# An RWKV-7 recurrence with a feed-forward network: the state's growth from weights of 40 columns, and the inverse decays turned ahead of minus x

## The chip, the cores and the metric

The kernel runs on one core of one Trainium2 chip. The metric is device time in microseconds (us) of one execution, the median of several runs. The engines are TensorE (PE, whose weight loads have a row of their own, PEld), VectorE (DVE), ScalarE (ACT), GpSimd (POOL) and SyncE (SP), which here only issues DMAs.

## The reference

A recurrence over 768 time steps for 4 batches and 8 heads of 40 elements, then a feed-forward network on its output:

```python
for t in range(S):
    kt, vt, rt = (k[:, :, t], v[:, :, t], r[:, :, t])
    wt, at, bt = (w[:, :, t], a[:, :, t], b[:, :, t])
    y[:, :, t] = np.einsum('bhd,bhde->bhe', rt, state)
    Sa = np.einsum('bhde,bhe->bhd', state, at)
    state_decay = state * wt[:, :, None, :] - np.einsum('bhd,bhe->bhde', Sa, bt)
    state = state_decay + np.einsum('bhd,bhe->bhde', vt, kt)
...
h = np.maximum(x @ w_in, 0.0)          # x: (3072, 320), w_in: (320, 2048)
return (h * h @ w_out)                 # w_out: (2048, 320)
```

The recurrence's inputs are 32-bit floats. The two weight matrices are 64-bit floats, which the kernel rounds to 32 bits on VectorE and ScalarE in its opening.

## The kernel before

**Chunks and slots.** Time is cut into 6 chunks of 128 steps for each of 4 batches: 24 chunks, numbered so that the batch runs fastest. Within a chunk the recurrence becomes matrix products: with cumulated decays (`dec`, its parts UP, DOWN and A) the inner dependence is a triangular system, which GpSimd inverts ahead of time (`solving`, results kept in memory and loaded as `T` or `blocks`). Heads go in pairs: a head has 40 elements, and a pair takes 128 partitions, the second head starting at 64 (`DP = 64`), so that 24 columns or rows after each head are padding. The tiles `in_k`, `in_v`, `in_b` and `minus_x` hold 8 heads of 64 columns of which 40 carry data and the rest are zeros.

**The chain of a chunk** (`chain`) is a generator whose steps the planner spreads among other work. Minus x is solved in two halves (`times_t`, copied to `minus_x` by ScalarE on line 658, two copies for each half). Then minus x is turned by four transposes on TensorE (line 671) into a bank of the pool ps_c, copied by ScalarE (line 673) to `xnT`, multiplied with `rT` and masked to `RX`. At the end come y (the products named RV,in_k and RX,in_b) and, for chunks 0 to 19, the state's growth: for each of 8 heads a product of v-side data (`in_v`) with weights `in_k`, and of `minus_x` with weights `in_b`, added in a bank `grown` of the pool ps_w (the profile names it ps_w). VectorE adds it to the state (line 701). The profile lists every matmul that goes through the helper `mm` under line 87, and each of these f32 matmuls as two loads and two matmuls; a transpose is one of each.

**The order.** Chunks 0 to 6 run in an opening whose order is written out as a list of words. From chunk 7 on, `sorted_slot(i, g, ch)` writes one slot for each chunk i: the chain of chunk i, the preparation of chunk j = i + 1 (turn r, v, k; scale k and b by the inverse decays), the decays of chunks further ahead (the generators `one` and `two`, in slots up to 14), and the feed-forward network's matmuls between. The code's order is each engine's order. `step` calls its arguments and then lets the list of delayed stores move on by one (`tick`).

**What the change touches.** `turn_down` (line 582) turns the inverse decays of chunk j by four transposes into a bank of ps_w, and `scale_kb` (line 588, VectorE) reads that bank. In the slot, `step(on(one), on(ch), of(turn_down))` runs a step of `one` (two products on VectorE, lines 387 and 388), then the transposes of minus x, then those of the inverse decays. Next on TensorE come the products of `rT` with the old state (`rT,sd`), 32 x 32 products named spares (slots up to 12), and the products of `rT` with `xnT`. The transposes of k (in_k, line 331) come before.

Of the kernel before, what the change touches and what calls it, by code (L numbers as in the profile page):

```python
# [17 lines left out]
def kernel(  # L18
# [24 lines left out]
    B, H, S, D = r.shape  # L43
# [7 lines left out]
    DP = 64  # L51
# [30 lines left out]
    def psum(pool):  # L82
        name = "ps_" + pool.name[-1]
        return pool.tile([128, 512], FP32, tag=name, name=name)

    def mm(o, l_, r_, start):
        nc.tensor.matmul(o, l_, r_, start=start, stop=True, skip_group_check=True)  # L87
# [4 lines left out]
    def new(name, shape, bufs):  # L92
        return work.tile(shape, FP32, tag=name, name=name, bufs=bufs)
# [4 lines left out]
    def later(fn, steps=2):  # L98
        line.append([steps, fn])

    def tick():
        for entry in line:
            entry[0] -= 1
        while line and line[0][0] <= 0:
            line.pop(0)[1]()
# [12 lines left out]
    class Ring:  # L118
# [6 lines left out]
        def next(self):  # L125
            self.at = (self.at + 1) % len(self.tiles)
            return self.tiles[self.at]
# [215 lines left out]
    def masked(name, bufs, l_, r_):  # L343
        res = []
        for p_ in products(l_, r_):
            t_ = new(name, [128, NP, 128], bufs)
            nc.vector.tensor_tensor(t_, p_, over4(upper), Alu.mult)  # L347
            res.append(t_)
        return res
# [252 lines left out]
    def begin(i, g):  # L602
        g["x"] = loaded.pop(i)
        g["up"], g["aT"] = g["dec"][:, UP], g["dec"][:, A_, :, :C]
# [27 lines left out]
    def chain(i, g):  # L632
        bb, c = order[i]
        st = states.tiles[bb]
        first, second_ = halves
        k_, b_, v_, rT = (g[x] for x in ("k", "b", "v", "rT"))

        x_ = psum(ps_c)[:, :DM].rearrange("t (h d) -> t h d", h=H)
        if c > 0:
            for f in range(2):  # L640
                for q in range(NP):
                    mm(x_[halves[f ^ q % 2], 2 * q:2 * q + 2], g["aT"][:, q, f * HC:(f + 1) * HC], st[:, q, :, :D], f == 0 and q < 2)
        for f in range(2):
            for n, (h, q, e, flip) in enumerate(heads):
                mm(x_[halves[f ^ flip], h], g["A"][e][:, q, f * HC:(f + 1) * HC], v_[:, h, :D], c == 0 and f == 0 and n < 2)
        xr = new("xr", [128, H, D], 1)
        nc.scalar.copy(xr, x_)  # L647
        yield
        T, N = g["T"], g["N"]
        xn = minus_x.next()  # L650

        def times_t(half):
            xs = psum(ps_c)[:, :NP * D].rearrange("p (n d) -> p n d", n=NP)
            for n, (h, q, e, flip) in enumerate(heads):
                rows = halves[half ^ flip]
                mm(xs[rows, n // 2], T[rows, order_of(h)], xr[rows, h], n < 2)
            for flip in range(2):
                nc.scalar.copy(flipped(xn)[halves[half], flip, :, :, :D], by_pair(xs[halves[half ^ flip]]))  # L658

        times_t(0)  # L660
        yield
        for h, q, e, flip in heads:
            mm(x_[halves[1 - flip], h], N[:, order_of(h)], xn[first, h, :D], False)
        for flip in range(2):
            nc.scalar.copy(flipped(xr)[halves[1 - flip], flip], flipped(x_)[halves[1 - flip], flip])
        yield
        times_t(1)
        yield
        p_ = psum(ps_c)
        for q in range(NP):  # L670
            nc.tensor.transpose(p_[:, q * 128:(q + 1) * 128], pair(xn, q), ident)  # L671
        xT = turned("xnT", 1)
        nc.scalar.copy(xT, quads(p_))
        yield
        y_ = quads(psum(ps_c))
        if c > 0:
            sd = g["sd"]
            for q in range(NP):
                mm(y_[:, q], sd[:, q].rearrange("p e d -> p (e d)"), rT[:, q], q == 0)
        yield  # L680
        rx = masked("RX", 2, xT, rT)
        yield

        for m_, rows in ((g["RV"], k_), (rx, b_)):
            for q in range(NP):
                for e in range(2):
                    mm(y_[e * DP:(e + 1) * DP, q], rows[:, 2 * q + e, :], m_[e][:, q], c == 0 and q == 0 and rows is k_)
        if c < NCH - 1:
            grown = psum(ps_w)[:, :NP * D].rearrange("p (q d) -> p q d", q=NP)
            for l_, r_ in ((k_, v_), (b_, xn)):  # L690
                for h in range(H):
                    mm(grown[h % 2 * DP:(h % 2 + 1) * DP, h // 2], l_[:, h, :], r_[:, h, :D], l_ is k_ and h < 2)
        n = i % GB
        if n == 0:
            tokens[i // GB] = new("tokens", [128, NP, GB * C], 2)
        t_ = tokens[i // GB][:, :, n * C:(n + 1) * C]
        nc.vector.tensor_tensor(t_, y_, g["up"][:, :, :C], Alu.mult)  # L697
        if c < NCH - 1:
            for e in range(2):
                rows = slice(e * DP, (e + 1) * DP)  # L700
                nc.vector.tensor_tensor(st[rows, :, e, :D], grown[rows], st[rows, :, e, :D], Alu.add)
            ended[bb] = new(f"end{bb}", [128, NP], 1)
            nc.scalar.copy(ended[bb], g["up"][:, :, C])
        if n == GB - 1:
            t_ = tokens[i // GB]

            def gather():
                for j, row, h, d, m_ in moves:
                    at = (h % 2) * DP + d
                    on_queue[0].dma_start(out=t_[row:row + m_, j], in_=t_[at:at + m_, h // 2])  # L710

            if i < LAID:
                waiting["m", i // GB] = gather
            else:
                later(gather, 1)
                later(lambda: gathered.add(i // GB), 2)
        yield
# [93 lines left out]
    def run(gen):  # L811
        for _ in gen:
            tick()
# [13 lines left out]
    def prepare(i, g=None, apart=False, steps=0):  # L827
        gen = early(i, g, apart)
        for _ in range(steps):
            next(gen)  # L830
            yield
        if i + 1 < len(order) and i + 1 not in early_loaded:
            load_early(i + 1)
        yield from gen
# [142 lines left out]
    def step(*what):  # L977
        for w_ in what:
            w_()
        tick()  # L980

    on = lambda gen: lambda: next(gen, None)

    def sorted_slot(i, g, ch):
        j = i + 1
        more = j < len(order)
        n = ready.setdefault(j, {}) if more else None
        made = [prepare(m_, apart=True) for m_ in ahead.get(i, ())]
        one, two = (made + [iter(()), iter(())])[:2]
        if j in inversions:  # L990
            n["joining"] = inversions.pop(j)
        early_join = more and "joining" in n
        joining = n.pop("joining") if early_join else inverses(j, n) if more else iter(())
        fine = more and unit_of[j] < FINE
        join = on(joining)
        of = lambda fn: (lambda: fn(j, n)) if more else (lambda: None)

        if more and "x" in n:
            n.update(up=n["dec"][:, UP], aT=n["dec"][:, A_, :, :C])
        elif more:  # L1000
            begin(j, n)
        step(second.make_quarter)
        if fine and not early_join:
            join()
        step(of(turn_rv), on(one), on(one))
        fetch_next(j + 1, "r")
        step(second.make_quarter)
        step(on(ch), of(decay_state))
        step(of(make_rv), second.thirds)
        step(on(ch), on(one))  # L1010
        if fine:
            join()
        step(second.whole)
        step(on(ch))
        step(on(one), of(turn_k))
        step(on(one), on(ch), of(turn_down))
        step(on(ch), of(scale_kb))
        if fine:
            join()
        step(on(ch), of(make_a), second.thirds, on(one))  # L1020
        fetch_next(j + 1, "v")
        step(of(turn_state), second.square, second.whole, on(two))
        if not early_join and not fine:
            join()
        run(ch)
        if more:
            begin_chain(j, n)
        loads(j + 1)
        step(second.square, second.make_quarter, on(two), on(two))
        if i in ahead and len(ahead[i]) > 1:  # L1030
            step(on(two), on(two))
        step(second.make_quarter, on(two))
        for gen in (one, two, joining):
            run(gen)

    for i in range(LAID, len(order)):
# [3 lines left out]
        ch = g["chain"]  # L1040
# [39 lines left out]
```

## Time and profile before

| what | value |
|---|---|
| runs shown | 949.51, 950.41, 963.28 us |
| median | 950.41 us |
| span of the profiled execution | 949.3 us |
| mean granted TensorE clock | 0.958 |
| instructions | 22557 |
| DMA | 103.37 MB, mean 109 GB/s |

The page gives the profiled execution's span, from its first to its last instruction, and no other time of it. A span says how long; the chain that ended last says what it was made of; the groups say how often an operation ran and how long one took; the timeline shows one slot instruction by instruction, with the idle time of an engine in brackets and what ended it. A group such as `128*64 128x40` has weights of 128 rows and 64 columns, and 40 moving columns. A TensorE matmul's length is its latency: matmuls overlap, so the distance from start to start tells what one costs in a row of them.

### The profile page before, as it was taken

The numbers are of one execution on the slowest core, as the hardware profiler recorded it, in microseconds if no ns is written. First come the engines' busy times: TensorE is split into PE (matmuls) and PEld (weight loads), VectorE is DVE, ScalarE is ACT, GpSimd is POOL, SyncE is SP. The second block draws the span as 40 slices with busy tenths as digits, with TensorE's granted clock in tenths as the row PEclk, the third lists the DMA queues.
The fourth block names the chain that finished last, engine by engine and source line by source line (L and its number), as shares of the span: only waits on it lengthen the run. The fifth ranks groups of instructions, "written<-read, shape, count | busy, mean of one in ns | idle before, by whom it ended". The sixth has DMA issues, their size and how long they took to land.

```text
span 949.3 us, 22557 instructions
## 1 busy us (share of the span) xinstructions
PE 896.9 (94%) x9116; PEld 719.2 (76%) x9116; DVE 462.1 (49%) x1131; ACT 284.8 (30%) x735; POOL 509.4 (54%) x935
## 2 busy tenths in 40 slices
PE   6578989879999999999999999999999999999998
PEld 4365656758787887888887888888888877887775
DVE  5927548788863355652664455544334331331110
ACT  3033334534532342342342232222221222222111
POOL 4568246064008786318999959999858870000000
PEclk9768988589999999999999999999999999999999
DMA  9788779856868477896846765604484154210000
GB/s 112 124 160 150 163 127 189 193 127 136 173 104 170 85 139 140 168 173 119 137 78 104 122 173 100 121 13 82 91 168 77 24 108 80 44 30 10 12 14 15
DMA packets 253266, 103.37 MB, mean 109 GB/s; under 512 B 234154, under 2 KB 240298, under 8 KB 252010
## 3 DMA queue, kind: packets, MB, share of 16 engines
q1 hardware_dynamic: 244709, 83.00, 49.2%
q0 software_dynamic: 3760, 17.10, 7.5%
q10 hardware_dynamic: 4693, 1.83, 0.9%
q8 instruction: 72, 1.18, 0.6%
q14 instruction: 32, 0.26, 0.1%
HBM read 69.00 MB, written 30.92 MB: 105 GB/s over the span
## 4 chain that ended last, share of the span: by engine, by line
PE 82%; DVE 6%; DMA 3%; ACT 3%; issue 2%; POOL 1%; SPq 1%; ACTq 0%; DVEq 0%; POOLq 0%
PE ps_f L87 40%; PE ps_w L87 17%; PE ps_c L87 14%; PE ps_w L331 5%; PE ps_f L264 2%; PE ps_c L671 2%; PE ps_c L598 1%; PE ps_w L582 1%; SPq L513 1%; DMA kept_q<-N 1%; DMA in_r<-in_r_dram 1%; DMA half_n<-kept_q 1%; ACT N L401 1%; DVE decay L381 1%; DVE decay L380 1%
## 5 line engine op out<-in xcount | busy, mean ns | idle before, releaser
L478 POOL TENSOR_TENSOR half_p<-half_n,half_t 128x462 f32<-128x462 f32 (+39 forms) x406 | 221.9, 547 | 74.3 <-DMA half_n<-kept_q 23.4
L480 POOL TENSOR_TENSOR half_t<-half_t,half_p 128x462 f32<-128x462 f32 (+39 forms) x406 | 237.7, 585 | 31.8
L87 PE MATMUL ps_f<-w_out,hid 128*128 128x320 f32 x768 | 218.4, 436 | 0.0
L87 PEld LDWEIGHTS ps_f<-w_out,hid 128*128 128x128 f32 x768 | 142.1, 190 | 54.0 <-issue 0.2
L87 PE MATMUL ps_f<-tokens,w_in 128*128 128x256 f32 x672 | 156.7, 387 | 0.0
L87 PEld LDWEIGHTS ps_f<-tokens,w_in 128*128 128x128 f32 x672 | 125.8, 192 | 18.7 <-issue 1.9
L769 DVE TENSOR_TENSOR hid<-hid 128x512 f32<-128x512 f32 x96 | 78.2, 853 | 50.6 <-ACT hid L762 50.2
L762 ACT ACTIVATE hid<-ps_f 128x512 f32<-128x512 f32 x84 | 49.5, 595 | 77.2 <-PE ps_f L87 77.1
L451 POOL DMA_DIRECT2D half_n<-kept_q x18 | 9.4, 526 | 88.4 <-DMA kept_m<-N 43.1
L372 DVE TENSOR_TENSOR_SCAN decay<-ps_w,ones 128x64 f32<-128x64 f32 x88 | 23.7, 270 | 67.0 <-PE ps_w L331 66.9
L697 DVE TENSOR_TENSOR tokens<-ps_c,dec 128x512 f32<-128x512 f32 x24 | 16.6, 691 | 79.6 <-PE ps_c L87 77.5
L347 DVE TENSOR_TENSOR RX<-ps_w,upper 128x512 f32<-128x512 f32 x48 | 30.8, 684 | 47.6 <-PE ps_w L87 47.4
L264 PE MATMUL ps_f<-ident 128*128 128x512 f32 (+3 forms) x108 | 49.8, 595 | 0.0
L347 DVE TENSOR_TENSOR RV<-ps_w,upper 128x512 f32<-128x512 f32 x48 | 30.9, 684 | 38.5 <-PE ps_w L87 38.2
L398 ACT COPY N<-ps_w 128x256 f32<-128x256 f32 x48 | 17.7, 368 | 94.4 <-PE ps_w L87 69.5
L87 PE MATMUL ps_f<-tokens,w_third 64*128 64x256 f32 x336 | 45.5, 381 | 0.1
L548 DVE TENSOR_TENSOR kvT<-ps_w,dec 128x512 f32<-128x512 f32 x24 | 16.4, 683 | 59.4 <-ACT minus_x L658 35.4
L87 PEld LDWEIGHTS ps_c<-xr,T 64*64 64x64 f32 x768 | 28.9, 143 | 20.7 <-issue 14.5
L570 DVE TENSOR_TENSOR f<-end,dec 128x4 f32<-128x4 f32 x20 | 7.5, 374 | 72.6 <-DMA dec<-kept_e 72.6
L331 PE MATMUL ps_w<-ident,in_ab 128*128 128x128 f32 x184 | 28.1, 298 | 11.9 <-DVE RV L347 10.0
L87 PE MATMUL ps_c<-xr,T 64*64 64x40 f32 x768 | 34.9, 237 | 3.8 <-ACT xr L647 2.6
L560 ACT COPY rT<-ps_w 128x512 f32<-128x512 f32 x24 | 14.0, 585 | 80.5 <-PE ps_w L331 80.4
(151 smaller groups left out, 1450.6 us busy)
## 6 DMA issues: line engine op xcount, KB each, us to landing
dec<-kept_e SPq DMA_DIRECT2D x22, 633.8 KB
kept_e<-decay SPq DMA_DIRECT2D x19, 633.8 KB
in_w<-in_w_dram SPq DMA_DIRECT2D x24, 160.0 KB
in_b<-in_b_dram SPq DMA_DIRECT2D x24, 160.0 KB
in_ab<-in_a_dram SPq DMA_DIRECT2D x24, 160.0 KB
in_r<-in_r_dram SPq DMA_DIRECT2D x24, 160.0 KB
in_v<-in_v_dram SPq DMA_DIRECT2D x24, 160.0 KB
out_dram<-o SPq DMA_DIRECT2D x24, 160.0 KB
```

Source lines behind the costliest of these rows:

```text
L87: nc.tensor.matmul(o, l_, r_, start=start, stop=True, skip_group_check=True)
L264: nc.tensor.matmul(fill_bank[:, :n * 128], ident, ident.unsqueeze(1).to_broadcast([128, n, 128]), start=True, stop=True, skip_group_check= ...
L331: nc.tensor.transpose(p_[:, q * 128:(q + 1) * 128], pair(x_, q), ident)
L347: nc.vector.tensor_tensor(t_, p_, over4(upper), Alu.mult)
L372: nc.vector.tensor_tensor_scan(up[:, q, MID + 1:C + 1], wT[:, q, MID:], ones, 1.0, Alu.mult, Alu.mult)
L398: nc.scalar.copy(plain, p_[:, ::2].rearrange("s h (f t) -> s f h t", f=2))
L478: eng.tensor_tensor(p_, part[:, at:at + m_].unsqueeze(1).to_broadcast([128, n, m_]), t3[:, :n, s:s + 1].to_broadcast([128, n, m_]), Alu.mult)
L480: eng.tensor_tensor(t3[:, :n, s + 1:], t3[:, :n, s + 1:], p_, Alu.subtract)
L671: nc.tensor.transpose(p_[:, q * 128:(q + 1) * 128], pair(xn, q), ident)
L697: nc.vector.tensor_tensor(t_, y_, g["up"][:, :, :C], Alu.mult)
L762: nc.scalar.activation(h_, p_.rearrange("p f t -> p (f t)"), Act.Relu)
L769: nc.vector.tensor_tensor(h_, h_, h_, Alu.mult)
```

## The change

Three places. The growth's weights are cut from 64 to 40 columns, so that the padding's rows of the output (40 to 63 and 104 to 127) are no longer written. The addition to the state covers the same 40 rows of each half. In the slot, the turning of the inverse decays gets a step of its own ahead of the step of `one` and the chain's turning of minus x.

```diff
             for l_, r_ in ((k_, v_), (b_, xn)):
                 for h in range(H):
-                    mm(grown[h % 2 * DP:(h % 2 + 1) * DP, h // 2], l_[:, h, :], r_[:, h, :D], l_ is k_ and h < 2)
+                    mm(grown[h % 2 * DP:h % 2 * DP + D, h // 2], l_[:, h, :D], r_[:, h, :D], l_ is k_ and h < 2)
...
             for e in range(2):
-                rows = slice(e * DP, (e + 1) * DP)
+                rows = slice(e * DP, e * DP + D)
                 nc.vector.tensor_tensor(st[rows, :, e, :D], grown[rows], st[rows, :, e, :D], Alu.add)
...
         step(on(one), of(turn_k))
-        step(on(one), on(ch), of(turn_down))
+        step(of(turn_down))
+        step(on(one), on(ch))
         step(on(ch), of(scale_kb))
```

On TensorE in slot 16, between the transposes of k and the products with the old state (dec_131 holds the decays of chunk 17, minus_x_132 is minus x; in brackets the counts that an instruction waits for):

```order
 L331 MATMUL ps_w<-ident,in_k_107 128x128 [waits DMAHW6_49]
 L331 MATMUL ps_w<-ident,in_k_107 128x128 x3
-L671 MATMUL ps_c<-ident,minus_x_132 128x128 [waits Activation_49] x2
-L671 MATMUL ps_c<-ident,minus_x_132 128x128 x2
 L582 MATMUL ps_w<-ident,dec_131 128x128 [waits DMAHW5_49]
 L582 MATMUL ps_w<-ident,dec_131 128x128 x3
+L671 MATMUL ps_c<-ident,minus_x_132 128x128 [waits Activation_49] x2
+L671 MATMUL ps_c<-ident,minus_x_132 128x128 x2
 L87 MATMUL ps_c<-rT,sd 128x128 [waits PE_49]
 L87 MATMUL ps_c<-rT,sd 128x128 x3
```

The four transposes of the inverse decays, which wait for a load alone, now stand ahead of the four of minus x, which wait for ScalarE. On TensorE at the same place of slot 10 (and alike in slots 7 to 14):

```order
 L331 MATMUL ps_w<-ident,in_k_107 128x128 [waits DMAHW0_49,DVE_49]
 L331 MATMUL ps_w<-ident,in_k_107 128x128 x3
-L671 MATMUL ps_c<-ident,minus_x_132 128x128 [waits Activation_49] x2
-L671 MATMUL ps_c<-ident,minus_x_132 128x128 x2
 L582 MATMUL ps_w<-ident,dec_131 128x128 [waits DMAHW7_49,DVE_49]
 L582 MATMUL ps_w<-ident,dec_131 128x128 x3
+L671 MATMUL ps_c<-ident,minus_x_132 128x128 [waits Activation_49] x2
+L671 MATMUL ps_c<-ident,minus_x_132 128x128 x2
```

Here the transposes of the inverse decays wait for VectorE besides, and those of minus x now stand behind that wait. On TensorE at the end of slot 16 (in_v_113 and in_k_106 are chunk 16's v and k, state_135 the state of chunk 17's batch):

```order
 L87 MATMUL ps_c<-RX,in_b_86 64x128 x6
-L87 MATMUL ps_w<-in_v_113,in_k_106 64x40 [waits PE_49]
-L87 MATMUL ps_w<-in_v_113,in_k_106 64x40 x7
-L87 MATMUL ps_w<-minus_x_132,in_b_86 64x40 x8
+L87 MATMUL ps_w<-in_v_113,in_k_106 40x40 [waits PE_49]
+L87 MATMUL ps_w<-in_v_113,in_k_106 40x40 x7
+L87 MATMUL ps_w<-minus_x_132,in_b_86 40x40 x8
 L87 MATMUL ps_c<-state_135,dec_131 64x80 [waits Activation_49]
 L87 MATMUL ps_c<-state_135,dec_131 64x80 x7
```

Nothing moves there: the same 16 matmuls have outputs of 40 rows in place of 64. The other engines and the DMA queues keep their order; from slot 15 on the turning of the state (L598) carries a wait on TensorE's own count that it did not carry.

## The prediction

> **What bounds the kernel now.** I read the page first, then the busy time by stages, then the groups by shape, and last the timeline of single slots. The page, busy time, slices and chain:
>
> ```profile
> span 949.3 us, 22557 instructions
> PE 896.9 (94%) x9116; PEld 719.2 (76%) x9116; DVE 462.1 (49%) x1131; ACT 284.8 (30%) x735; POOL 509.4 (54%) x935
> PE   6578989879999999999999999999999999999998
> PE 82%; DVE 6%; DMA 3%; ACT 3%; issue 2%; POOL 1%; SPq 1%; ACTq 0%; DVEq 0%; POOLq 0%
> ```
>
> TensorE (PE) carries 82% of the chain that ends last. The stages show where a microsecond saved on PE is a microsecond saved (columns: stretch, its length, busy time of PE, PEld, DVE, ACT and POOL, granted clock, DMA share, GB/s):
>
> ```profile
> 0.00:100.00 100.00, 69.68 (x586) 50.52 (x587) 63.18 (x218) 29.40 (x80) 63.72 (x184) 0.81 0.84 138
> 200.00:300.00 100.00, 92.87 (x982) 75.63 (x979) 72.71 (x194) 41.15 (x109) 36.11 (x87) 0.97 0.70 142
> 300.00:400.00 100.00, 99.02 (x1160) 82.80 (x1159) 50.24 (x142) 34.27 (x97) 66.83 (x176) 1.00 0.75 133
> 600.00:700.00 100.00, 100.00 (x1085) 82.33 (x1084) 42.23 (x62) 22.99 (x54) 84.06 (x98) 1.00 0.47 90
> ```
>
> From about 300 us on PE does not rest and its clock is 1.00. Before that, in the opening, it waits for loads, VectorE and ScalarE, and a faster matmul there may only wait longer.
>
> The span is 949.3 us, 1.1 below the median of the three runs shown (950.41) and 0.2 below the fastest. I make the sum against the span and add 1.1.
>
> **Part A, weights of 40 columns.** State's growth is 16 matmuls in each of 20 slots (chunks 0 to 19). Each is two loads and two matmuls in the trace, so 32 pairs a slot. The groups by shape, with their mean time for one, then slot 16 on the timeline (start, length, engine, line, operation):
>
> ```profile
> L87 PE MATMUL ps_c<-xr,T 64*64 64x40 f32 x768 | 34.9, 237 | 3.8 <-ACT xr L647 2.6 <-ACT xr L665 1.2
> L87 PE MATMUL ps_c<-state,dec 128*64 128x80 f32 x320 | 15.1, 236 | 0.0
> L87 PE MATMUL ps_w<-in_v,in_k 128*64 128x40 f32 x320 | 13.2, 229 | 0.0
> L87 PE MATMUL ps_w<-spares 32*32 32x32 f32 x448 | 10.1, 195 | 2.4 <-DVE spares L520 2.4
> 652.34 0.66 PE L87 MATMUL ps_c<-xr,T 64*64 64x40 f32 x16
> 664.22 0.61 PE L87 MATMUL ps_w<-in_v,in_k 128*64 128x40 f32 x16
> 664.66 0.64 PE L87 MATMUL ps_w<-minus_x,in_b 128*64 128x40 f32 x16
> 665.12 0.75 PE L87 MATMUL ps_c<-state,dec 128*64 128x80 f32 x16
> 665.35 0.66 DVE L701 TENSOR_TENSOR state<-ps_w,state 64x160 f32<-64x160 f32 x2 [0.22 <-PE ps_w L87]
> 456.67 0.69 PE L87 MATMUL ps_w<-spares 32*32 32x32 f32 x32
> ```
>
> The 229 ns of one matmul is its latency; matmuls overlap, and what counts is the step from one to the next. From 664.22 to 665.12 the 32 pairs take 0.90 us, 28.1 ns a pair. What sets that step? Not the moving columns: the group with 80 of them steps by (0.75 - 0.236)/15 = 34.3 ns, and half of that, 17.1 ns, would do for 40. Not the rows of the weights: 64 x 64 weights step by (0.66 - 0.237)/15 = 28.2 ns, the same with half the rows. What is left is the load of 64 columns. The 32 x 32 weights step by (0.69 - 0.195)/31 = 16.0 ns, so 32 columns fewer are worth 12.1 ns. By a straight line between the two, 40 columns step by 16.0 + 12.1 x 8/32 = 19.0 ns, still above the 17.1 of the moving side. That saves 9.1 ns a pair, 0.29 us a slot. No weights in this trace have a width between 32 and 64, so the bounds are 28.1 (no gain) and 17.1 ns (11.0 a pair), and the line is my choice because 40 lies near its lower end.
>
> How many of the 20 slots keep it? Of the 14 growths in slots 6 to 19, three are given back: those ahead of slots 7, 8 and 10, where PE next waits for a load that is issued before the growth ends (rows under B). Of the six in the opening I count three, as PE is busy 70 to 93% there. So 14 x 0.29 = 4.1 us; all 20 would be 5.8.
>
> The state's addition (L701) goes from 64 to 40 partitions with the same 160 elements in each; I cost it at nothing: 0.66 us a slot on an engine that is busy 42 of 100 us, and nothing reads that state before slot i + 3, when it is decayed and turned for the batch's next chunk.
>
> **Part B, inverse decays ahead of minus x.** Four transposes (L582) pass four others (L671). They issue no DMA, and no row moves on any other engine or queue. L671 waits for the second of two ScalarE copies of minus x (L658). Slot 16, where that shows, then slot 13, where the copies come early, and L671 of the first and last slot of the kind of 16:
>
> ```profile
> 652.94 0.66 PE L331 MATMUL ps_w<-ident,in_k 128*128 128x128 f32 x4
> 653.07 0.60 ACT L658 COPY minus_x<-ps_c 64x160 f32<-64x160 f32 x2
> 653.43 0.84 PE L671 MATMUL ps_c<-ident,minus_x 128*128 128x128 f32 x4
> 654.11 0.60 PE L582 MATMUL ps_w<-ident,dec 128*128 128x128 f32 x4
> 654.54 1.06 PE L87 MATMUL ps_c<-rT,sd 128*128 128x128 f32 x8
> 655.53 1.16 PE L87 MATMUL ps_w<-rT,xnT 40*128 40x128 f32 x16
> ...
> 557.20 0.60 PE L331 MATMUL ps_w<-ident,in_k 128*128 128x128 f32 x4
> 557.64 0.60 PE L671 MATMUL ps_c<-ident,minus_x 128*128 128x128 f32 x4
> 558.08 0.60 PE L582 MATMUL ps_w<-ident,dec 128*128 128x128 f32 x4
> 558.27 0.59 ACT L673 COPY xnT<-ps_c 128x512 f32<-128x512 f32 x1 [1.27 <-PE ps_c L671]
> 558.51 1.06 PE L87 MATMUL ps_c<-rT,sd 128*128 128x128 f32 x8
> ...
> 622.58 0.84 PE L671 MATMUL ps_c<-ident,minus_x 128*128 128x128 f32 x4
> 836.67 0.84 PE L671 MATMUL ps_c<-ident,minus_x 128*128 128x128 f32 x4
> ```
>
> Unhindered, the three groups of four take 558.51 - 557.20 = 1.31 us; in slot 16 they take 654.54 - 652.94 = 1.60. The 0.29 is the wait for the copies, which end at 653.67. With L582 first, PE has 0.44 us of work from 653.38 to 653.82, past the copies' end, and the wait is gone. Slots 15 to 22, eight of them, have this form (the two last rows): 8 x 0.29 = 2.3 us.
>
> What is late next? The copy of the turned minus x (L673) and the products that read it. They lose 0.44 us of cover, the length of L582. By slot 13, the copy starts 0.63 us after L671 and takes 0.59, so it ends 1.22 us after L671's start; PE has 0.44 + (655.53 - 654.54) = 1.43 us of work there. It stays covered, by 0.2 us.
>
> Now the slots where L582 itself waits. While decays are still prepared (slots up to 14) it waits for VectorE, which shows in slots 7 and 10; in slot 8 it is L671 that waits long:
>
> ```profile
> 340.71 0.17 DVE L570 TENSOR_TENSOR f<-end,dec 128x4 f32<-128x4 f32 x1 [5.31 <-DMA dec<-kept_e]
> 344.87 0.32 DVE L381 TENSOR_TENSOR_SCAN decay<-ps_w,decay,ones 128x63 f32<-128x63 f32 x1
> 345.24 0.42 PEld L582 LDWEIGHTS ps_w<-ident,dec 128*128 128x128 f32 x4 [0.24 <-DVE decay L381]
> 449.60 0.76 DVE L570 TENSOR_TENSOR f<-end,dec 128x4 f32<-128x4 f32 x1 [4.55 <-DMA dec<-kept_e]
> 454.81 0.32 DVE L381 TENSOR_TENSOR_SCAN decay<-ps_w,decay,ones 128x63 f32<-128x63 f32 x1
> 455.19 0.66 PE L582 MATMUL ps_w<-ident,dec 128*128 128x128 f32 x4
> 380.34 0.91 ACT L522 ACTIVATE T<-blocks,which 128x256 f32<-128x256 f32 x2 [3.12 <-DMA blocks<-kept_t]
> 382.58 0.86 PE L671 MATMUL ps_c<-ident,minus_x 128*128 128x128 f32 x4 [0.36 <-ACT minus_x L658]
> 383.27 0.60 PE L582 MATMUL ps_w<-ident,dec 128*128 128x128 f32 x4
> ```
>
> In slots 7 and 10 VectorE starts late, behind the load of the decays (waits of 5.31 and 4.55 us), and L582 starts 0.05 us after its last scan ends (345.19, 455.13). In slot 8 ScalarE starts late behind the load of the solved blocks (3.12). Today L671 fills that wait. After the change L671 stands behind it, with all of PE's queue, and runs afterwards: 0.44 us lost in each. In slot 8 L582 fits wholly into L671's wait: 0.44 won. Part B is 2.3 + 0.44 - 0.88 = 1.9 us; its bounds are -0.9 (the eight waits return elsewhere, slot 8 wins nothing) and +2.7 (VectorE comes earlier in slots 7 and 10).
>
> One row gains a wait on PE's own count, the turning of the state (L598) from slot 15 on; what it waits for has long run by then, so nothing.
>
> **Sum.** 4.1 + 1.9 = 6.0 us. 949.3 - 6.0 = 943.3 of span, 944.4 as a run.
>
> **Rivals.** *The load takes 40 columns as long as 64* (the array is filled in blocks, and 40 needs as many as 64). No row speaks against it, as none has such a width. A is 0: 948.5.
>
> *Pairs cannot follow each other faster than some 25 ns.* The in_v,in_k group steps by (0.61 - 0.229)/15 = 25.4, close to such a floor; the step of 16.0 with 32 x 32 weights speaks against it, if those are not a case of their own. A is 14 x 32 x 2.7 ns = 1.2 us: 947.3. The Trainium skill has this rule: "TensorE: Matmul & The Clock Gate", in the section "Wait — 56ns, not 53.3ns?", states that matmuls never start less than about 25 ns apart however few columns they have. By its figure A would be an estimated 1.4 us; the 16.0 ns row of this trace disagrees with it.
>
> *The copy of the turned minus x becomes the wait.* If it ends 0.3 us later than I work out, as ScalarE's copies did in slot 8, slots 13 to 22 lose 0.1 each, 1.0 us in all: 945.4.
>
> *Slower: an odd width costs the overlap of the two column halves.* Heads alternate between output rows 0 and 64, and the step of 34.3 ns for 80 columns shows the halves running side by side. If 40-wide weights no longer do, 40 columns alone need the 34.3, 6.2 ns more than now: 14 x 32 x 6.2 = 2.8 us lost against 1.9 won, 951.3; if the load of 19.0 ns is uncovered too, 53.3 a pair and 959.8. It decides from a step of 28.1 + 4.3 = 32.4 ns on. The even steps of 64 x 64 and 128 x 64 weights speak against it, as does that the halves stay at rows 0 and 64.
>
> **Chances.** My forecast 0.52; no gain from A 0.18; the floor 0.11; the copy 0.08; slower 0.07; everything kept (all 20 slots and B at 2.7: 5.8 + 2.7 = 8.5, so 941.9) 0.04. Range 941.0 to 951.0: below, A at 17.1 ns a pair in all 20 slots (7.0) with B at 2.7 is 940.7; above, it ends at the mild slower case. Two per cent, about what a measurement of this kernel can tell from no change, is 19 us: no case reaches it either way. I leave 0.02 for each side, 0.96 for within.
>
> **What would show it.** In the changed profile the growth's two groups should last from 0.90 to about 0.61 us, start to start, with no new gap before state,dec. L671 should be 0.60 long in slots 15 to 22, in_k to rT,sd 1.31 there, and 0.44 longer than now in slots 7 and 10. A start-to-start of 0.8 shows the floor, 0.9 no gain. I am wrong if PE shows new waits at rT,xnT, or if the opening ends later than before.

## The result and the profile after

| kernel | median of the runs, us | lowest to highest | ratio to before, 95% interval |
|---|---|---|---|
| before | 950.96 (18 runs) | 948.12 to 963.28 | |
| changed | 945.71 (18 runs) | 939.15 to 957.12 | 0.993 (0.9909 to 0.9951) |

By the interval the changed kernel is faster by 0.5 to 0.9%, a difference of less than 2%. The ratio compares the runs without one slow run of each kernel (963.28 and 957.12 us) and is not the quotient of the two medians, which is 0.9945. The median lies 1.3 us above the forecast of 944.4 and inside the range. The profiled execution of the changed kernel took 950.48 us, more than 16 of its 18 runs, so its span must not be held against the one before. The page of the changed kernel, span, busy time, slices and chain:

```profile
span 948.8 us, 22557 instructions
PE 896.5 (94%) x9116; PEld 718.6 (76%) x9116; DVE 463.1 (49%) x1131; ACT 285.4 (30%) x735; POOL 508.8 (54%) x935
PE   6667989889999999999999999999999999999998
PE 82%; DVE 8%; ACT 3%; DMA 3%; issue 2%; SPq 1%; POOL 0%; ACTq 0%; DVEq 0%; POOLq 0%
```

The page says almost nothing: one span is 0.5 us shorter than the other, and the shares are alike. What the change did shows only in single slots. The growth, in the groups by shape and in slot 16 of the changed kernel:

```profile
L87 PE MATMUL ps_w<-in_v,in_k 128*40 128x40 f32 x320 | 10.2, 209 | 0.0
666.43 0.47 PE L87 MATMUL ps_w<-in_v,in_k 128*40 128x40 f32 x16
666.73 0.48 PE L87 MATMUL ps_w<-minus_x,in_b 128*40 128x40 f32 x16
667.03 0.75 PE L87 MATMUL ps_c<-state,dec 128*64 128x80 f32 x16
```

From start to start the 32 pairs now take 667.03 - 666.43 = 0.60 us, 18.8 ns a pair, against 0.90 and 28.1. The turned decays, in slot 16 and then in slot 7 of the changed kernel:

```profile
655.38 0.65 PE L331 MATMUL ps_w<-ident,in_k 128*128 128x128 f32 x4
655.52 0.60 ACT L658 COPY minus_x<-ps_c 64x160 f32<-64x160 f32 x2
655.88 0.60 PE L582 MATMUL ps_w<-ident,dec 128*128 128x128 f32 x4
656.31 0.60 PE L671 MATMUL ps_c<-ident,minus_x 128*128 128x128 f32 x4
656.75 1.06 PE L87 MATMUL ps_c<-rT,sd 128*128 128x128 f32 x8
657.74 0.49 PE L87 MATMUL ps_w<-rT,xnT 40*128 40x128 f32 x4
...
349.96 0.60 PE L331 MATMUL ps_w<-ident,in_k 128*128 128x128 f32 x4
351.06 0.33 DVE L381 TENSOR_TENSOR_SCAN decay<-ps_w,decay,ones 128x63 f32<-128x63 f32 x1
351.44 0.66 PE L582 MATMUL ps_w<-ident,dec 128*128 128x128 f32 x4 [0.88 <-DVE decay L381]
351.94 0.60 PE L671 MATMUL ps_c<-ident,minus_x 128*128 128x128 f32 x4
352.38 1.06 PE L87 MATMUL ps_c<-rT,sd 128*128 128x128 f32 x8
```

In slot 16 the copies of minus x end at 656.12, while L582 runs, and L671 is 0.60 long instead of 0.84. In slot 7 minus x has long been copied, but it stands behind L582, and L582 behind VectorE's last scan: 0.88 us in which TensorE waits.

**How to compare two executions here.** I use three marks, the starts of `rT,sd` in slots 7, 13 and 22. Before, then changed:

```profile
345.74 1.06 PE L87 MATMUL ps_c<-rT,sd 128*128 128x128 f32 x8
558.51 1.06 PE L87 MATMUL ps_c<-rT,sd 128*128 128x128 f32 x8
837.78 1.06 PE L87 MATMUL ps_c<-rT,sd 128*128 128x128 f32 x8
```

```profile
352.38 1.06 PE L87 MATMUL ps_c<-rT,sd 128*128 128x128 f32 x8
562.10 1.06 PE L87 MATMUL ps_c<-rT,sd 128*128 128x128 f32 x8
837.35 1.06 PE L87 MATMUL ps_c<-rT,sd 128*128 128x128 f32 x8
```

The changed kernel comes out of the opening 6.6 us later, which the prediction named as a sign of being wrong, and by slot 22 it is 0.4 us ahead. From slot 7 to 22 it takes 484.97 us instead of 492.04. After slot 22 both are alike. So two questions were left: whether the late opening is the change's doing, and which part of it gave which share of the 7.1 us.

### The profile page after: what moved, and what is told of

Its sections match the earlier page's. It is cut to its first block, busy times and chain, and to the rows that moved or that the text cites. A ratio compares the mean times of both kernels' runs of the same rounds, so it can differ in the third digit from the quotient of the medians.

```text
span 948.8 us, 22557 instructions
## 1 busy us (share of the span) xinstructions
PE 896.5 (94%) x9116; PEld 718.6 (76%) x9116; DVE 463.1 (49%) x1131; ACT 285.4 (30%) x735; POOL 508.8 (54%) x935
## 4 chain that ended last, share of the span: by engine, by line
PE 82%; DVE 8%; ACT 3%; DMA 3%; issue 2%; SPq 1%; POOL 0%; ACTq 0%; DVEq 0%; POOLq 0%
PE ps_f L87 40%; PE ps_w L87 16%; PE ps_c L87 14%; PE ps_w L331 6%; PE ps_f L264 3%; PE ps_c L598 1%; PE ps_c L671 1%; DMA in_r<-in_r_dram 1%; PE ps_w L582 1%; SPq L513 1%; DVE half_t L480 1%; DVE half_t L478 1%; DMA dec<-kept_e 1%; ACT N L401 1%; DVE decay L381 1%
## 5 line engine op out<-in xcount | busy, mean ns | idle before, releaser
L769 DVE TENSOR_TENSOR hid<-hid 128x512 f32<-128x512 f32 x96 | 80.9, 882 | 50.6 <-ACT hid L762 50.2
L264 PE MATMUL ps_f<-ident 128*128 128x512 f32 (+3 forms) x108 | 53.2, 630 | 0.0
L331 PE MATMUL ps_w<-ident,in_ab 128*128 128x128 f32 x184 | 28.1, 298 | 10.6 <-DVE RV L347 8.6
```

The source lines that it names most:

```text
L264: nc.tensor.matmul(fill_bank[:, :n * 128], ident, ident.unsqueeze(1).to_broadcast([128, n, 128]), start=True, stop=True, skip_group_check= ...
L331: nc.tensor.transpose(p_[:, q * 128:(q + 1) * 128], pair(x_, q), ident)
L769: nc.vector.tensor_tensor(h_, h_, h_, Alu.mult)
```

## The experiments

**The same kernels again.** No edit: the changed kernel twice more, the kernel before once more.

> The changed kernel once more, to part what the change does from what the opening does by itself. Measured from the start of the products rT,sd in slot 7 to their start in slot 22, the kernel before took 837.78 - 345.74 = 492.04 us and the changed one 837.35 - 352.38 = 484.97. Theory: this stretch is fixed by the order on TensorE, so it is 485.0 again within 0.3, and slot 7's mark (352.38 in the first profile) moves by several us from one execution to the next. Rival: the change delays the opening, so that the mark lies at 350 to 354 again.

> The kernel before once more, for one question: how much does the opening move by itself? Theory: the mark of slot 7 (start of rT,sd; 345.7 in the first profile) lies somewhere between 342 and 352, as far apart as those of the changed kernel (352.4 and 350.7). Rival: it lies within 1 us of 345.7, and the changed kernel's later marks are the change's doing.

> The changed kernel a third time: mark of slot 7 (352.4 and 350.7 before) between 342 and 352 by the theory, 350 to 353 by the rival.

The marks of the changed kernel's first repeat, of the second, and of the repeat of the kernel before:

```profile
350.72 1.06 PE L87 MATMUL ps_c<-rT,sd 128*128 128x128 f32 x8
561.92 1.06 PE L87 MATMUL ps_c<-rT,sd 128*128 128x128 f32 x8
837.17 1.06 PE L87 MATMUL ps_c<-rT,sd 128*128 128x128 f32 x8
```

```profile
345.55 1.06 PE L87 MATMUL ps_c<-rT,sd 128*128 128x128 f32 x8
557.27 1.06 PE L87 MATMUL ps_c<-rT,sd 128*128 128x128 f32 x8
832.52 1.06 PE L87 MATMUL ps_c<-rT,sd 128*128 128x128 f32 x8
```

```profile
351.93 1.06 PE L87 MATMUL ps_c<-rT,sd 128*128 128x128 f32 x8
563.46 1.06 PE L87 MATMUL ps_c<-rT,sd 128*128 128x128 f32 x8
842.72 1.06 PE L87 MATMUL ps_c<-rT,sd 128*128 128x128 f32 x8
```

The mark of slot 7 lies at 345.7 and 351.9 for the kernel before, at 352.4, 350.7 and 345.6 for the changed one: the opening moves by 6 us by itself, and the rival falls. So a late opening in one execution, the prediction's sign of being wrong, was no sign at all. What does not move is the stretch from slot 13 to slot 22: 279.27 and 279.26 before, 275.25, 275.25 and 275.25 changed. The stretch from slot 7 to 13 moves: 212.8 and 211.5 before, 209.7, 211.2 and 211.7 changed. My expectation that all of slots 7 to 22 would be steady within 0.3 us was wrong (486.5 and 487.0 in the repeats).

What moves there are waits in slots 8, 9 and 10. From the start of in_k to that of `rT,sd`, each of slots 8 to 14 takes 1.31 us where nothing is late. That is so in all of them in two executions: the repeat of the kernel before, which takes 842.72 - 351.93 = 490.79 us from slot 7 to 22, and the first of the changed kernel, 484.97. The 5.82 between these two are 13 growths (slots 7 to 19) of 0.30 and eight slots of 0.24 (part B): 3.90 + 1.92. The other 1.3 of the 7.1 us between the first two profiles are waits that the first execution before has in slots 8 and 10 (2.09 and 1.82 instead of 1.31) and its repeat has not. In the changed kernel's repeats slot 10 took 2.79 in the first and slot 9 took 3.30 in the second, which makes their 486.5 and 487.0.

In 12 timed runs the changed kernel's repeat had a median of 946.63, ratio 0.9926 (0.9894 to 0.9959).

**Each part alone.** The growth alone, in which the order of the slot is the old one:

```diff
-                    mm(grown[h % 2 * DP:(h % 2 + 1) * DP, h // 2], l_[:, h, :], r_[:, h, :D], l_ is k_ and h < 2)
+                    mm(grown[h % 2 * DP:h % 2 * DP + D, h // 2], l_[:, h, :D], r_[:, h, :D], l_ is k_ and h < 2)
...
-                rows = slice(e * DP, (e + 1) * DP)
+                rows = slice(e * DP, e * DP + D)
```

> Only the weights of 40 columns; the old order in the slot. Theory: 0.30 us for each growth, 13 of them between the marks of slots 7 and 22: 488.1 us between the marks, and some 4 to 5 us less in all than the kernel before. Rival: in slots 8 and 10 the saving is given back to the loads that are awaited there: 488.7.

> The growth alone once more. Its opening has the same instructions in the same order on every engine as the changed kernel's. Theory: its mark of slot 7 (340.5 before) moves by several us. Rival: it is at 340 to 341 again, and the order in the slot changes the opening in a way that the order of instructions does not show.

The order alone, with weights of 64 columns:

```diff
-        step(on(one), on(ch), of(turn_down))
+        step(of(turn_down))
+        step(on(one), on(ch))
```

> Only the inverse decays ahead of minus x; weights of 64 columns as before. Theory: the wait for minus x goes in slots 8, 10 and 15 to 22 (0.74 + 0.51 + 8 x 0.24 = 3.2): 488.9 us between the marks, and slot 7 loses 0.4 to 0.9 between the start of in_k and that of rT,sd (1.53 before). Rival, as forecast: slot 10 loses 0.44 instead, 489.8 between the marks.

Marks of slots 13 and 22, of the growth alone and then of the order alone:

```profile
550.52 1.06 PE L87 MATMUL ps_c<-rT,sd 128*128 128x128 f32 x8
827.69 1.06 PE L87 MATMUL ps_c<-rT,sd 128*128 128x128 f32 x8
```

```profile
564.30 1.06 PE L87 MATMUL ps_c<-rT,sd 128*128 128x128 f32 x8
841.66 1.06 PE L87 MATMUL ps_c<-rT,sd 128*128 128x128 f32 x8
```

In the steady stretch the growth alone takes 277.17 us, 2.10 less than before, which is 7 growths of 0.30. The order alone takes 277.36, 1.91 less, which is 8 slots of 0.24. Together that is 4.01, and the changed kernel has 279.26 - 275.25 = 4.01: here the parts add up exactly.

Between slots 7 and 13 late loads hide them. There the growth alone takes 210.1 us in one execution and 218.8 in the other, the order alone 216.6. The longest waits of TensorE from 340 to 870 us say why, in the growth's second execution, then in the order alone (who waited for whom, us in total, times, longest):

```profile
PE ps_c L671 <- ACT minus_x L658: 6.7, 2, 6.3
```

```profile
PE ps_c L671 <- ACT minus_x L658: 3.5, 2, 3.1
```

The long wait of each falls in slot 9. In the growth's second execution, ScalarE stood there behind a load that landed late:

```profile
422.52 0.91 ACT L522 ACTIVATE T<-blocks,which 128x256 f32<-128x256 f32 x2 [9.08 <-DMA blocks<-kept_t]
```

That wait comes in some executions of either order, not in all; a comparison of whole runs averages over it. From slot 7 to 22 I had expected 488.1 us of the growth alone and 488.9 of the order alone; they took 487.22 and 495.99, and 493.93. Without what the steps from slot 7 to 10 take beyond those of the two executions with nothing late, it is 486.9 (both times) and 488.9: 490.79 less 13 x 0.30, and less 8 x 0.24. In whole runs the growth alone took 945.61 (8 runs, ratio 0.9929, 0.9898 to 0.9960), the order alone 950.03 (12 runs, 0.9956, 0.9926 to 0.9987). The growth alone thus can't be told from the changed kernel: what the order adds to it shows between the marks, not in the totals.

The growth alone repeats the point on the opening: its mark of slot 7 lay at 340.47 and at 344.92, with the same instructions.

**Where the new order does harm.** The changed kernel with the old order in slot 7, and with the old order in slots 7 to 14:

```diff
-        step(of(turn_down))
-        step(on(one), on(ch))
+        if i == LAID:
+            step(on(one), on(ch), of(turn_down))
+        else:
+            step(of(turn_down))
+            step(on(one), on(ch))
```

> The changed kernel, but slot 7 keeps the old order. Theory: the inverse decays wait in slot 7 for the last scan of VectorE, and ahead of minus x they hold up TensorE there; with the old order, in_k to rT,sd in slot 7 takes 1.5 to 2.0 us (2.42 in the changed kernel), the rest stays (485.0 between the marks), so this beats both kernels by 0.4 to 0.6 us against the changed one, less than the runs can tell. Rival: the scans are late for another reason and slot 7 takes 2.4 either way.

For the second kernel the condition is `i < 15`. (`LAID` is 7.)

> Weights of 40 columns everywhere, the new order only in slots 15 to 22, where no decays are prepared and the inverse decays wait for no scan. Theory: slots 15 to 22 give 8 x 0.24 = 1.9 us as in the changed kernel (in_k to rT,sd 1.37 instead of 1.61), the marks of slots 14 and 22 stand as far apart as there; slots 7 to 10 go as with the old order, by whatever loads come late; in all 943.7, about 2 us below the growth alone (945.6) and below both kernels. Rival: what slots 8 and 10 gained with the new order is missing, 945 to 946.

From the start of in_k to that of `rT,sd`, slot 7 took 1.97 us in the first of these kernels and 1.90 in the second. Over all executions with 40 moving columns in the growth it took 1.31 to 2.50 us with the old order (six of them) and 1.93 to 2.77 with the new one (six). The means lie some 0.6 us apart, but the two overlap, so the 1.97 and 1.90 decide nothing by themselves. The waits of the changed kernel's first execution and of its first repeat, from 340 to 870 us, show the mechanism:

```profile
PE ps_w L582 <- DVE decay L381: 0.9, 1, 0.9
```

```profile
PE ps_w L582 <- DVE decay L381: 2.1, 2, 1.3
```

The wait for the scan is there with the old order too. In slot 7 of the repeat of the kernel before it is even longer:

```profile
351.44 0.65 PE L582 MATMUL ps_w<-ident,dec 128*128 128x128 f32 x4 [0.97 <-DVE decay L381]
351.93 1.06 PE L87 MATMUL ps_c<-rT,sd 128*128 128x128 f32 x8
```

What the order sets is the work that is left after the wait. Here `rT,sd` starts 0.49 us after L582; in slot 7 of the changed kernel, where L671 still has to run, 352.38 - 351.44 = 0.94. So the new order costs 0.45 us where the scan is late, and the rest of the 0.6 is the scatter of six executions against six. The second of the changed repeat's two waits falls in slot 10, where in_k to `rT,sd` took 2.79 us instead of 1.31. Of these 1.48 the order again accounts for 0.44 (0.93 from L582 to `rT,sd`), the late scan for the rest. In the changed kernel's other two executions slot 10 had no wait. In slot 8 the new order left none in any execution (1.31 each time), and the old one 0 to 0.8 us; how much of that is the order's doing, and how much a load that came earlier, these runs don't part.

The kernel with the old order in slot 7 took 484.93 us from slot 7 to 22, the 485.0 expected. The one with the new order from slot 15 on kept the steady stretch (275.26). In all it took 946.08 us (12 runs, 0.9930, 0.9891 to 0.9969), the one with the old order in slot 7 944.35 (12 runs, 0.9924, 0.9892 to 0.9956). Neither can be told from the changed kernel; the 943.7 that I expected of the former did not come.

**What sets the step of a pair.** Weights of 48 and 56 columns, and half the moving columns with weights of 64 and of 40 (the last two leave half of each head's state without growth). The first edit (56 alike), then the fourth:

```diff
-mm(grown[h % 2 * DP:h % 2 * DP + D, h // 2], l_[:, h, :D], r_[:, h, :D], l_ is k_ and h < 2)
+mm(grown[h % 2 * DP:h % 2 * DP + 48, h // 2], l_[:, h, :48], r_[:, h, :D], l_ is k_ and h < 2)
...
-mm(grown[h % 2 * DP:h % 2 * DP + D, h // 2], l_[:, h, :D], r_[:, h, :D], l_ is k_ and h < 2)
+mm(grown[h % 2 * DP:h % 2 * DP + D, h // 2, :D // 2], l_[:, h, :D], r_[:, h, :D // 2], l_ is k_ and h < 2)
```

> The changed kernel with growth weights of 48 columns (8 of them padding). Theory, a load as long as its columns: 32 pairs step by 16.0 + 12.1 x 16/32 = 22.1 ns, so the growth takes 0.71 us from the start of in_v,in_k to that of state,dec (0.60 with 40 columns, 0.90 with 64). Rival, the load goes by blocks: 0.60 or 0.90, like one of its neighbours.

> The changed kernel with growth weights of 56 columns. Theory: 25.1 ns a pair, 0.80 us for the growth. Rival, blocks: 0.90 or 0.60.

> The kernel before, with only 20 of the 40 moving columns in the growth: half of each head's state does not grow. Theory, the load sets the step: the growth stays at 0.90 us although half the moving columns are gone. Rival, the moving columns set it: 0.45 to 0.60 us.

> The changed kernel with 20 moving columns in the growth: half of each head's state does not grow. Theory, the load still sets the step at 40 columns (19.0 ns against 17.1 of the moving side): 0.60 us as with 40 moving columns. Rival, a step that the moving side bounds: clearly less, down to 0.55 us, or 0.80 if no pair may follow another in less than 25 ns.

Slot 16 of the four, in the same order:

```profile
662.24 0.52 PE L87 MATMUL ps_w<-in_v,in_k 128*48 128x40 f32 x16
662.94 0.75 PE L87 MATMUL ps_c<-state,dec 128*64 128x80 f32 x16
```

```profile
666.48 0.57 PE L87 MATMUL ps_w<-in_v,in_k 128*56 128x40 f32 x16
667.28 0.75 PE L87 MATMUL ps_c<-state,dec 128*64 128x80 f32 x16
```

```profile
663.67 0.60 PE L87 MATMUL ps_w<-in_v,in_k 128*64 128x20 f32 x16
664.58 0.75 PE L87 MATMUL ps_c<-state,dec 128*64 128x80 f32 x16
```

```profile
658.63 0.46 PE L87 MATMUL ps_w<-in_v,in_k 128*40 128x20 f32 x16
659.23 0.75 PE L87 MATMUL ps_c<-state,dec 128*64 128x80 f32 x16
```

The growth takes 0.60, 0.70, 0.80 and 0.90 us at 40, 48, 56 and 64 columns: a straight line, 0.10 us for 8 columns, 3.1 ns a pair. It does not care for the moving columns: 0.91 us with 20 of them on weights of 64, 0.60 on weights of 40. So the columns of the weights set the step, evenly over widths 8 apart and not in larger blocks, and these pairs have no floor at 25 ns. That it is the load of these columns is the reading that fits. The rows of the output are as many as the columns of the weights, and no run parts the two; but half the moving columns write half as much, and that changed nothing.

## Why the prediction was right, point by point

- **The base.** I added 1.1 us to the span. Runs whose spans are known lie 1.7 above them (950.48 and 948.8 for the changed kernel, 955.92 and 954.2 for the one before). The profiled execution of before then took about 951.0 by an estimate, and 951.0 - 6.0 = 945.0: half of the 1.3 us by which the median missed is this step.
- **Part A, the size.** 0.29 us a growth was predicted, 0.30 measured; the step of 19.0 ns came out at 18.8. The straight line between 32 and 64 columns, a choice then, is now measured at 48 and 56.
- **Part A, what is kept.** All 13 growths from slot 7 on are kept where no load is late, those ahead of slots 8 and 10 too: the steps from mark to mark of slots 7 to 10 take 37.24, 37.20 and 34.27 us in the repeat of before, 36.93, 36.89 and 33.98 in the changed kernel. I had taken the late loads of one execution for a property of the kernel, but they fall in slot 8, 9 or 10, or in none. For the growth ahead of slot 7 and the six of the opening, of which I kept three, the runs show nothing: the opening moves by several us.
- **Part B, the eight slots.** Predicted 0.29 each, measured 0.24. The step that was mis-sized is the unhindered time of the three groups: I took slot 13's 1.31 us, but in slot 16 the transposes of k follow products of another shape, and from in_k's start to the next group 0.49 to 0.50 us pass in either kernel (652.94 to 653.43 before, 655.38 to 655.88 changed), not 0.44. Those 0.06 us were no wait for minus x. L671 alone, 0.84 against 0.60, gave the right number.
- **Part B, what is late next.** The copy of the turned minus x stayed covered: `rT,sd` to `rT,xnT` takes 0.99 us, as before, so that rival fell.
- **Part B, the slots with scans.** The mechanism was right: L582 waits for the scan and holds L671 up, and where it does, that costs 0.44 to 0.45 us, as predicted. How often it does was not to be had from one execution: in slot 7 in all three of the changed kernel, in slot 10 in one of three. That slot 10 lost nothing in the first execution, against a forecast of 0.44, was luck with a load. That slot 8 wins 0.44 is not shown.
- **The sum.** 6.0 us were predicted. The medians lie 5.25 us apart; the ratio of 0.993 on about 951 is 6.7 us (4.7 to 8.7). Of it 5.8 us are shown between slots 7 and 22: 3.9 from 13 growths and 1.9 from eight slots. What the seven growths before slot 7 (at most 2.1), the loss in slot 7 and the late loads leave can't be told apart by these runs. That the sum came so close is in part luck: for slots 7 to 22 it had 3.2 + 2.3 = 5.5, with too few growths (11 of 13) and too much for part B, and its part for the time before slot 7 was never seen.
- **The rivals.** No gain from the load fell, since the growth takes 0.60 us. The floor of 25 ns fell. The 25.4 ns that spoke for it came from the mean length of a matmul; from start to start the same group steps by (664.66 - 664.22)/16 = 27.5. The Trainium skill's rule ("TensorE: Matmul & The Clock Gate", section "Wait — 56ns, not 53.3ns?") does not hold for these pairs at 18.8 ns. The loss of overlap fell too, as the step of 18.8 ns lies below even the 34.3 that 40 columns without overlap would take.

## What to carry to other kernels

Where small matmuls each bring their own weights, the step from one to the next may go by the columns of the weights, and padding there is then paid in full, while here 20 moving columns fewer saved nothing: compare groups of other widths in the trace before and after. Work moved ahead of a wait fills it only if it waits for nothing later itself; look at each place where the same code runs, since here it filled the wait in eight slots and lengthened one in slot 7. When an opening moves by several us from execution to execution, compare a late stretch between two marks, which here repeated to 0.01 us. And a late load in one trace is not yet the kernel's: take a second trace before building a sum on it.

## What the runs showed of the hardware

A pair of load and matmul with f32 weights of 128 rows steps by 18.8, 21.9, 25.0 and 28.1 ns at 40, 48, 56 and 64 columns, while the granted clock was 1.00: 0.39 ns a column, on a rest of some 3 ns. The Trainium skill ("TensorE: Matmul & The Clock Gate", section "LDWEIGHTS (loading the stationary operand)") gives 1/1.2 ns a column, whatever the rows. That it is the columns agrees with these runs; the slope here is less than half of it. And the same program left its opening at 340.5 us in one execution and 344.9 in another, and at 345.7 and 351.9 in the kernel before, without a change of any instruction.
